# Threshold attention and a gated FFN on one core: half-size units of plain products, new slot tables, and one more dependency in the planner's account

## The chip, the cores and the metric

The kernel runs on one core of one Trainium2 chip, in float32. The metric is device time in microseconds of one execution. Times are medians of several runs; the profile is of one execution with its own time. "PE" is TensorE, "DVE" is VectorE, "ACT" is ScalarE, "POOL" is GpSimd, and "SP" is the sync engine, which issues most DMA transfers.

## What is computed

Attention over 8 batches of 8 heads with 576 positions of 64 elements, in which scores below the row's maximum less `tau` are dropped, and then a gated feed-forward block over the 4608 tokens (512 to 1536 to 512).

```python
def _attn_ref(q, k, v, tau):
    scale = 1.0 / np.sqrt(q.shape[-1])
    scores = scale * np.matmul(q, k.transpose(0, 1, 3, 2))
    thresh = np.max(scores, axis=-1, keepdims=True) - tau
    scores = np.where(scores >= thresh, scores, -1000000000.0)
    scores = scores - np.max(scores, axis=-1, keepdims=True)
    attn = np.exp(scores)
    attn = attn / (np.sum(attn, axis=-1, keepdims=True) + 1e-09)
    return np.matmul(attn, v)

def _moe_ref(x, w_gate, w_val, w_out):      # x: heads joined, 4608 x 512
    g = x @ w_gate
    silu = g * (1.0 / (1.0 + np.exp(-g)))
    val = x @ w_val
    return silu * val @ w_out
```

## The kernel before

The first 135 us are a head: the first batch's attention is done tile by tile, and the FFN's weights are loaded, converted and joined. After that the kernel is a run of 84 **slots**, 12 for each of the seven batches 1 to 7 (four head pairs times three groups of query rows). The FFN of batch b-1 runs inside the slots of batch b, and what is left over runs in a tail from about 1150 us on.

**One slot** is one round of the loop at the end of the kernel:

- `slot_scores` puts the score product on PE (line 1719, tile `sc`): 64 rows of the profile, written to two PSUM tiles of a pool of two, one for each head. So the next slot's scores can begin only when this slot's readers have let go of both tiles.
- `slot_rest` queues the softmax. DVE takes maxima (1740, 1742), the two halves of a row's maximum are joined either on DVE (1748, 1749) or on ACT (1754, then 1758 on DVE), ACT makes the threshold (1761) and six exps (1765), and DVE makes six masked products with their sums, the **masks** (1767). The masks are the last readers of the score tiles. Their six units are (head, u) for u = 0, 1, 2. Then sums are exchanged on ACT (1775), DVE makes the reciprocals (1780, 1781), ACT (1793) or POOL (1790) scales the units, and DVE transposes them (1795) for the product with V.
- In every third slot `attend` does that product for the head pair before (line 1816, tile `xa`). It waits for all nine transposes of its segment of three slots.
- `block_part` puts a share of the FFN's products on PE between this slot's scores and the next slot's. This share is what covers the softmax's latency.

**Which share a slot gets** is written in tables by slot number s (or by kk, the slot within a batch). For slots 0 to 8, `PLAIN` says how many steps of the generators `plain_group` are taken. These are the plain products of the first chunk (the FFN of batch 0): one step is one gate product `pg` or one value product `pv`, 8 matmuls of 128x128x256 (line 1200; float32 matmuls stand in the profile as two rows each, so 16 rows). `CH0` says how many output products `po` (line 1269, 12 rows each) slots 8 to 12 take. For slots 13 to 21, which carry the second chunk, `GV_FIRST` says how many products of `gates_and_values` (line 993, tiles `pa`, `pb`, `pe`, 8 rows each, a Strassen-like scheme of seven products for each of six groups) are taken. Later batches use `GV`, and from batch 3 on the output products are nested (line 1472, `px`, and 1481, `py`). `POOLED` and `FIRST_POOLED` say how many of a slot's scalings go to POOL, and `MAX_BY_ACT` and `FIRST_MAX_BY_ACT` list the slots whose maxima are joined on ACT. The "FIRST" tables hold for slots 0 to 23.

**What sets the order on the other engines** is `Plan`. PE's order is the order of the program. Every other instruction is a `job` with an engine, a planned duration, dependencies and a rank. Whenever PE work is added, `Plan.run` moves the account of time on and emits, engine by engine, the job that can start, lower rank first. Emitted order is final: each engine runs its queue in that order on the chip and waits where an operand isn't ready. The account's dependencies only decide the order; the waits that the program really has are put in by the framework from the tiles' accesses. In the account before, an exp of unit u = 2 follows the masks of u = 0 and 1 of its head, and an exp of u = 1 follows no mask.

`Deep.inner_sums` makes the sums of operands for the nested output products on POOL (line 846; `o` is the operand's number), and its jobs have rank 1 for o = 1 and 5 and rank 2 otherwise.

In slots 0 to 6 remaining pieces of the output weights are converted between the slots' jobs: ACT 873 and 876 (the first waits for the load of its piece, line 279 or 864), DVE 883 and 885, POOL 887.

Of the kernel before, what the change touches and what calls it, by code (L numbers as in the profile page):

```python
# [112 lines left out]
def kernel(  # L113
# [11 lines left out]
    nc = tc.nc  # L125
    P = 128
# [3 lines left out]
    NCC = DM // P  # L130
# [58 lines left out]
    wgv = big[:, 0:2 * NCC * DFF].rearrange("p (m c f) -> p m c f", m=2, c=NCC)  # L189
# [588 lines left out]
    job, pe = plan.job, plan.pe  # L778
# [194 lines left out]
    MM = 0.4325  # L973
# [215 lines left out]
    def plain_group(t, g, n_bufs):  # L1189

        x = xts["full", t]

        def mul(mat, name):
            hold = take(name)

            def fn():
                ps = hold.rows()
                for i in range(2):
                    for c in range(NCC):
                        nc.tensor.matmul(ps[:, i], wgv[:, mat, c, (2 * g + i) * P:(2 * g + i + 1) * P], x[:, c, :],  # L1200
                                         start=(c == 0), stop=(c == NCC - 1))

            return hold, pe(2 * NCC * MM, fn, *hold.deps)

        hold, m = mul(0, "pg")
        (u, u_old), (n, n_old) = turn_of(u_bufs), turn_of(n_bufs)
        ps = hold.rows()
        tj = job("ACT", 0.6, lambda: nc.scalar.activation(n.ap, ps, AF.Tanh, scale=0.5), m, *n_old, rank=1)
        cj = job("ACT", 0.6, lambda: nc.scalar.activation(u.ap, ps, AF.Copy, scale=0.5), m, *u_old, rank=1)
        hold.read_by(tj, cj)  # L1210
        hold.done(False)
        yield
        hold, m = mul(1, "pv")
        ht, pv = hall[:, t, g], hold.rows()
        vj = job("DVE", 0.7, lambda: nc.vector.scalar_tensor_tensor(out=ht, in0=n.ap, scalar=1.0, in1=pv, op0=ALU.add, op1=ALU.mult),
                 tj, m, rank=1)
        n.jobs = [vj]
        hold.read_by(vj)
        hold.done(False)
        gated[0, t, g] = mj = job("POOL", 1.3, pool_tt(ht, ht, u.ap, ALU.mult), vj, cj, rank=1)  # L1220
        u.jobs = [mj]
        yield
# [178 lines left out]
    class Deep:  # L1401
# [43 lines left out]
        def inner_sums(self, o, a, place, ready, *deps):  # L1445

            a11, a21, a12, a22 = quarters(a)
            flat = place if len(place.shape) == 2 else place.rearrange("p f n -> p (f n)")
            s1, s2, s3, s4 = (flat[:, n * QW:(n + 1) * QW].rearrange("p (f q) -> p f q", q=P) for n in range(4))
            tt, eng, took = (dve_tt, "DVE", 0.49) if tail[0] else (pool_tt, "POOL", 1.0)  # L1450
            rank = 1 if o in (1, 5) else 2
            j3 = job(eng, took, tt(s3, a11, a21, ALU.subtract), *ready, *deps, rank=rank)
            j1 = job(eng, took, tt(s1, a21, a22, ALU.add), *ready, *deps, j3, rank=rank)
            j2 = job(eng, took, tt(s2, s1, a11, ALU.subtract), j1, rank=rank)
            j4 = job(eng, took, tt(s4, a12, s2, ALU.subtract), j2, rank=rank)
            self.inner[o] = [(a11, ready), (a12, ready), (s4, [j4]), (a22, ready), (s1, [j1]), (s2, [j2]), (s3, [j3])]
# [267 lines left out]
    def slot_rest(seg, t, pss, mark, pooled, max_by_act, rank):  # L1724
        m = 2 * NU3
        mx, nm, th, ri, tot = statistics("mx", "nm", "th", "ri", "tot")
        sm = sums[0]
        sums.rotate(1)
        old_sums, sum_users[0] = sum_users[0], []
        sum_users.rotate(-1)  # L1730
        tiles = [(h, u) for u in range(NU3) for h in range(2)]
        at_of = lambda h, u: seg["p"] + (2 * (NU3 * t + u) + h) * SH
        scs = {(h, u): pss[h][:, u, 0:SH] if u < 2 else pss[h][:, :, SH:SH + SQ] for h, u in tiles}
        flat = {x: pall[:, at_of(*x):at_of(*x) + SH] for x in tiles}
        ps = {x: y if x[1] < 2 else y.rearrange("p (a n) -> p a n", a=2) for x, y in flat.items()}
        n_of = lambda h, u: NU3 * h + u
        rs = []
        for h, tile_ in enumerate(pss):
            n = n_of(h, 0)
            rs.append(job("DVE", 0.72, lambda n=n, tile_=tile_: nc.vector.tensor_reduce(  # L1740
                out=mx[:, n:n + 2, 0], in_=tile_[:, :, 0:SH], axis=AX.X, op=ALU.max, negate=True), mark, rank=0))
            rs.append(job("DVE", 0.42, lambda n=n, tile_=tile_: nc.vector.tensor_reduce(  # L1742
                out=mx[:, n + 2:n + 3, 0], in_=tile_[:, :, SH:SH + SQ], axis=AX.XY, op=ALU.max, negate=True), mark, rank=0))

        def largest():
            for g in range(NG):
                o = g ^ 1
                nc.vector.tensor_reduce(out=mx[g * G:(g + 1) * G, 0:m, 1], in_=mx[o * G:(o + 1) * G, 0:m, 0:1], axis=AX.X, op=ALU.max)
            nc.vector.tensor_reduce(out=nm[:, 0:m], in_=mx[:, 0:m, :], axis=AX.X, op=ALU.min)

        def others():
            for g in range(NG):
                o = g ^ 1
                nc.scalar.copy(mx[g * G:(g + 1) * G, 0:m, 1], mx[o * G:(o + 1) * G, 0:m, 0])

        if max_by_act:
            oj = job("ACT", 0.78, others, *rs, rank=0)
            nj = job("DVE", 0.18, lambda: nc.vector.tensor_reduce(out=nm[:, 0:m], in_=mx[:, 0:m, :], axis=AX.X, op=ALU.min), oj, rank=0)
        else:
            nj = job("DVE", 0.82, largest, *rs, rank=0)  # L1760
        ej = job("ACT", 0.25, lambda: nc.scalar.activation(th[:, 0:m], nm[:, 0:m], AF.Identity, bias=cut, scale=-1.0), nj, rank=0)
        masks = {}
        for h, u in tiles:
            x, n = (h, u), n_of(h, u)
            ej = job("ACT", 0.42, lambda x=x, n=n: nc.scalar.activation(ps[x], scs[x], AF.Exp, bias=nm[:, n:n + 1]), ej,  # L1765
                     *((masks[h, 0], masks[h, 1]) if u == 2 else ()), rank=0)
            masks[x] = job("DVE", 0.45, lambda x=x, n=n: nc.vector.scalar_tensor_tensor(  # L1767
                out=ps[x], in0=scs[x], scalar=th[:, n:n + 1], in1=ps[x], op0=ALU.is_ge, op1=ALU.mult, accum_out=sm[:, n, 0:1]),
                ej, *old_sums, rank=0)
        sc_users[:] = masks.values()  # L1770

        def exchange():
            for g in range(NG):
                o = g ^ 1
                nc.scalar.copy(sm[g * G:(g + 1) * G, 0:m, 1], sm[o * G:(o + 1) * G, 0:m, 0])  # L1775

        xj = job("ACT", 0.78, exchange, *masks.values(), rank=1)

        def total():
            nc.vector.tensor_reduce(out=tot[:, 0:m], in_=sm[:, 0:m, :], axis=AX.X, op=ALU.add)  # L1780
            nc.vector.reciprocal(out=ri[:, 0:m], in_=tot[:, 0:m])  # L1781

        rj = job("DVE", 0.36, total, xj, rank=1)
        sum_users[-1].append(rj)
        for u in range(NU3):
            scaled = []
            for h in range(2):
                x, n = flat[h, u], n_of(h, u)
                if h and u < pooled:
                    scaled.append(job("POOL", 1.02, lambda x=x, n=n: nc.gpsimd.tensor_scalar(  # L1790
                        out=x, in0=x, scalar1=ri[:, n:n + 1], scalar2=None, op0=ALU.mult), rj, rank=1))
                else:
                    scaled.append(job("ACT", 0.46, lambda x=x, n=n: nc.scalar.activation(x, x, AF.Copy, scale=ri[:, n:n + 1]), rj, rank=rank))  # L1793
            both = pall[:, at_of(0, u):at_of(0, u) + 2 * SH]
            seg["turned"].append(job("DVE", 0.72, lambda both=both: nc.vector.transpose(out=both, in_=both), *scaled, rank=rank))  # L1795
# [118 lines left out]
    NS = NU3 * NP  # L1914
    LAST_GV, LAST_PLAIN = 9, 8
    GV = {1: 2, 2: 7, 3: 4, 4: 5, 5: 6, 6: 5, 7: 6, 8: 6, 9: 0}
    GV_FIRST = {1: 4, 2: 5, 3: 4, 4: 6, 5: 7, 6: 3, 7: 5, 8: 6, 9: 1}
    CH = {0: 2, 1: 3, 10: 4, 11: 4}
    POOLED = {1: 3, 3: 2, 6: 3, 7: 2, 11: 1}
    MAX_BY_ACT = (0, 3, 5, 6, 8, 9, 10)  # L1920
    FIRST_POOLED = {0: 2, 1: 2, 4: 1, 6: 1, 7: 2, 8: 2, 10: 1, 11: 1, 12: 2, 13: 2, 14: 3, 15: 3, 17: 2, 18: 1, 19: 3, 20: 1, 21: 1, 22: 1, 23: 3}
    FIRST_MAX_BY_ACT = (0, 1, 2, 3, 6, 9, 12, 15, 16, 18, 20, 21)
    CD = {0: 1, 1: 1, 9: 2, 10: 2, 11: 2}
    PLAIN = {0: 2, 1: 2, 2: 3, 3: 1, 4: 2, 5: 3, 6: 1, 7: 2}
    CH0 = {8: 3, 9: 2, 10: 4, 11: 3, 12: 2}

    def begin_outputs(c):
        if c < DEEP:
# [39 lines left out]
    for s, (n, x) in enumerate((n, x) for n in range(len(halved)) for x in range(NU3)):  # L1968
        seg = halved[n]
        i, t = seg["i"], seg["tiles"][x]  # L1970
# [30 lines left out]
        if s in WS:  # L2001
            g, place = WS[s]
# [75 lines left out]
```

## Time and profile before

| | us |
|---|---|
| median of 3 runs (1369.13 to 1370.78) | 1370.28 |
| the profiled execution | 1371.92 |
| its span, first to last instruction | 1369.8 |
| PE, of the chain that ended last | 89% |
| mean granted TensorE clock | 0.997 |

The chain that ended last is PE for nearly nine tenths; its largest lines are the products of `gates_and_values` (993, 39% in three tiles), the nested products (1472, 12%), the scores (1719, 10%) and `xa` (1816, 9%). The plain products of line 1200 are 4%. PE's busy share by fortieths of the span is 89 to 96% over the first 171 us and 97 to 100% from there to the last slice. A timeline's row has start, duration, engine, line, operation and tiles, and in brackets the engine's idle time before it with what ended it. A row's duration on PE is not its cost where rows overlap; the distance of starts is.

### The profile page before, as it was taken

To read this page: it belongs to the slowest core of one execution; us is meant where nothing else is said; L and a number is where in the kernel's file an instruction comes from. 1 tells how busy PE (TensorE), PEld (TensorE's weight loads), DVE (VectorE), ACT (ScalarE), POOL (GpSimd) and SP (SyncE) were. 2 spreads that over 40 slices of the span, in tenths; PEclk is the share of its full clock that TensorE was granted. 3 is DMA by queue.
4 is the path that set the end of the run, shared out by engine and by line. 5 is a ranking of instruction groups with operands and counts; after the bars stand their busy time and mean duration, and the time that the engine had idled before them with its cause. 6 is when DMAs were issued, how large, how long until landed. Compare 5 with 4: busy or idle time off the path is not lost.

```text
span 1369.8 us, 39206 instructions
## 1 busy us (share of the span) xinstructions
PE 1350.8 (99%) x15590; PEld 1120.1 (82%) x15590; DVE 1069.4 (78%) x2815; ACT 876.6 (64%) x2277; POOL 717.6 (52%) x665
## 2 busy tenths in 40 slices
PE   9899999999999999999999999999999999999998
PEld 7777787778778778887888888878887788999998
DVE  6788888887887777777778877877777776788786
ACT  6798777666756767676767766776767774330330
POOL 1689597664564669534974287437943592000000
PEclk9999999999999999999999999999999999999999
DMA  7762424455523541555154513553165403424411
GB/s 168 185 204 74 103 55 124 133 137 144 174 52 126 144 116 38 171 147 141 36 157 130 151 47 128 139 144 92 37 191 144 113 27 136 161 78 147 151 65 32
DMA packets 208294, 162.32 MB, mean 119 GB/s; under 512 B 166128, under 2 KB 180464, under 8 KB 202736
## 3 DMA queue, kind: packets, MB, share of 16 engines
q1 hardware_dynamic: 203920, 158.86, 41.1%
q8 instruction: 124, 2.03, 0.6%
q10 hardware_dynamic: 4192, 0.95, 0.3%
q14 instruction: 58, 0.48, 0.1%
HBM read 138.28 MB, written 21.50 MB: 117 GB/s over the span
## 4 chain that ended last, share of the span: by engine, by line
PE 89%; DVE 4%; DMA 2%; POOL 2%; issue 1%; SPq 1%; ACT 1%; ACTq 0%; DVEq 0%; POOLq 0%
PE pb L993 18%; PE pa L993 12%; PE px L1472 12%; PE sc L1719 10%; PE xa L1816 9%; PE pe L993 9%; PE po L1269 5%; PE py L1481 5%; PE pg L1200 2%; PE pv L1200 2%; PE sc L1154 2%; SPq L367 1%; DMA vall<-in_v_dram 1%; PE pe L1154 1%; PE sc L438 1%
## 5 line engine op out<-in xcount | busy, mean ns | idle before, releaser
L1767 DVE SCALAR_TENSOR_TENSOR pall<-sc,th,pall 128x288 f32<-128x288 f32 x504 | 244.1, 514 | 59.3 <-ACT pall L1765 44.1
L993 PE MATMUL pb<-xall,big 128*128 128x256 f32 x1152 | 273.6, 381 | 0.0
L1765 ACT ACTIVATE pall<-sc,nm 128x288 f32<-128x288 f32 x504 | 231.4, 496 | 34.9 <-DVE pall L1767 34.8
L993 PEld LDWEIGHTS pb<-xall,big 128*128 128x128 f32 x1152 | 216.9, 191 | 30.5 <-issue 2.5
L1795 DVE STREAM_TRANSPOSE pall<-pall 128x576 f32<-128x576 f32 x252 | 188.9, 763 | 51.3 <-ACT pall L1793 34.6
L1793 ACT ACTIVATE pall<-pall,ri 128x288 f32<-128x288 f32 x415 | 189.4, 527 | 26.4 <-DVE ri L1781 25.8
L846 POOL TENSOR_TENSOR hall<-hall,tmp 128x512 f32<-128x512 f32 x80 | 102.2, 1277 | 158.5 <-DVE hall L1046 141.7
L993 PE MATMUL pa<-xall,big 128*128 128x256 f32 x768 | 183.5, 382 | 0.0
L993 PEld LDWEIGHTS pa<-xall,big 128*128 128x128 f32 x768 | 143.3, 190 | 21.8 <-issue 3.4
L1740 DVE TENSOR_REDUCE mx<-sc 128x2 f32<-128x576 f32 x168 | 125.0, 744 | 35.6 <-PE sc L1719 35.1
L1719 PE MATMUL sc<-kT,qT 64*32 64x288 f32 (+1 forms) x5376 | 147.4, 345 | 3.0 <-DVE pall L1767 1.4
L1719 PEld LDWEIGHTS sc<-kT,qT 64*32 64x32 f32 x5376 | 96.6, 106 | 56.9 <-issue 19.8
L993 PE MATMUL pe<-xall,big 128*128 128x256 f32 x576 | 137.3, 382 | 0.1
L1816 PE MATMUL xa<-pall,vall 64*32 64x288 f32 x4032 | 129.0, 404 | 0.1
L993 PEld LDWEIGHTS pe<-xall,big 128*128 128x128 f32 x576 | 108.7, 190 | 16.9 <-issue 2.9
L1790 POOL TENSOR_SCALAR pall<-pall,ri 128x288 f32<-128x288 f32 x89 | 88.7, 1007 | 63.9 <-DVE ri L1781 60.7
L1816 PEld LDWEIGHTS xa<-pall,vall 64*32 64x32 f32 x4032 | 75.8, 107 | 45.6 <-issue 5.3
L1775 ACT COPY sums<-sums 32x6 f32<-32x6 f32 x336 | 66.6, 198 | 41.3 <-DVE pall L1767 36.6
L1045 ACT ACTIVATE vall<-tmp 128x512 f32<-128x512 f32 x96 | 60.2, 630 | 28.8 <-POOL tmp L846 10.7
L1481 PE MATMUL py<-wo,hall 128*128 128x256 f32 x336 | 74.8, 380 | 0.0
L1742 DVE TENSOR_REDUCE mx<-sc 128x1 f32<-128x288 f32 x168 | 74.7, 445 | 0.0
L846 POOL TENSOR_TENSOR tmp<-tmp 128x512 f32<-128x512 f32 x36 | 45.9, 1274 | 53.6 <-ACT tmp L1068 53.6
(258 smaller groups left out, 2485.1 us busy)
## 6 DMA issues: line engine op xcount, KB each, us to landing
big<-sums_hbm SPq DMA_DIRECT2D x42, 1024.0 KB, 5.2
big<-sums_hbm SPq DMA_DIRECT2D x48, 768.0 KB, 4.8
vall<-in_v_dram SPq DMA_DIRECT2D x112, 144.0 KB, 3.1
out_dram<-big SPq DMA_DIRECT2D x32, 256.0 KB, 2.8
qT<-in_q_dram SPq DMA_DIRECT2D x112, 72.0 KB, 4.7
kT<-in_k_dram SPq DMA_DIRECT2D x112, 72.0 KB, 3.1
wo<-in_moe_w_gate_dram SPq DMA_DIRECT2D x16, 384.0 KB, 4.0
wo<-in_moe_w_val_dram SPq DMA_DIRECT2D x16, 384.0 KB, 4.7
```

Of the source, the lines that this page charges most:

```text
L846: return lambda: nc.gpsimd.tensor_tensor(out=out, in0=a, in1=b, op=op)
L993: nc.tensor.matmul(ps[:, i], w[:, k_, i * P:(i + 1) * P], x[:, k_, :], start=first and i == k_ == 0, stop=True, skip_group_check=True)
L1472: nc.tensor.matmul(ps, a[:, f, :], ws[n][:, f, :], start=bank_ not in begun, stop=True, skip_group_check=True)
L1481: nc.tensor.matmul(ps(), a[:, f, i * P:(i + 1) * P], operands[o][:, f, :], start=first and f == 0, stop=True, skip_group_check=True)
L1719: nc.tensor.matmul(pss[h][(slice(g * G, (g + 1) * G), *part)], qT[hs, col:col + G], kT[hs, c * SH + keys[0]:c * SH + keys[1]], start=True, ...
L1740: rs.append(job("DVE", 0.72, lambda n=n, tile_=tile_: nc.vector.tensor_reduce(out=mx[:, n:n + 2, 0], in_=tile_[:, :, 0:SH], axis=AX.X, op= ...
L1765: ej = job("ACT", 0.42, lambda x=x, n=n: nc.scalar.activation(ps[x], scs[x], AF.Exp, bias=nm[:, n:n + 1]), ej, *((masks[h, 0], masks[h, 1] ...
L1767: masks[x] = job("DVE", 0.45, lambda x=x, n=n: nc.vector.scalar_tensor_tensor(out=ps[x], in0=scs[x], scalar=th[:, n:n + 1], in1=ps[x], op0 ...
L1790: scaled.append(job("POOL", 1.02, lambda x=x, n=n: nc.gpsimd.tensor_scalar(out=x, in0=x, scalar1=ri[:, n:n + 1], scalar2=None, op0=ALU.mul ...
L1793: scaled.append(job("ACT", 0.46, lambda x=x, n=n: nc.scalar.activation(x, x, AF.Copy, scale=ri[:, n:n + 1]), rj, rank=rank))
L1795: seg["turned"].append(job("DVE", 0.72, lambda both=both: nc.vector.transpose(out=both, in_=both), *scaled, rank=rank))
L1816: nc.tensor.matmul(holds[a].ap()[x * G:(x + 1) * G, 0:SH].rearrange("d (i q) -> d i q", q=G), vr[rs, h, j, ds], p[rs, h, :, j, :], start=( ...
```

## The change

- `plain_group` hands out its two products in halves: `mul` makes one of the two rows i of the PSUM tile (4 matmuls), and the generator yields between them, so that a step of the plain stage is half as long as before. The waits on the PSUM bank stand on the first half.
- `PLAIN` counts halves now (32 in all, for 16 products before) and is laid out anew. `CH0` starts in slot 7 and takes one less in slot 10. `GV_FIRST`, `FIRST_POOLED` and `FIRST_MAX_BY_ACT` have other entries; `GV_FIRST` has 41 steps as before.
- In the planner's account, an exp of unit u follows the mask of unit u-1 of its head: for u = 1 that is new, for u = 2 the mask of u = 0 is no longer named.
- In `Deep.inner_sums`, o = 1 has rank 0 (before: 1).

```diff
@@ plain_group
-        def mul(mat, name):
-            hold = take(name)
-
+        def mul(hold, mat, i):
             def fn():
                 ps = hold.rows()
-                for i in range(2):
-                    for c in range(NCC):
-                        nc.tensor.matmul(ps[:, i], wgv[:, mat, c, (2 * g + i) * P:(2 * g + i + 1) * P], x[:, c, :],
-                                         start=(c == 0), stop=(c == NCC - 1))
-
-            return hold, pe(2 * NCC * MM, fn, *hold.deps)
-
-        hold, m = mul(0, "pg")
+                for c in range(NCC):
+                    nc.tensor.matmul(ps[:, i], wgv[:, mat, c, (2 * g + i) * P:(2 * g + i + 1) * P], x[:, c, :],
+                                     start=(c == 0), stop=(c == NCC - 1))
+
+            return pe(NCC * MM, fn, *(() if i else hold.deps))
+
+        hold = take("pg")
+        mul(hold, 0, 0)
+        yield
+        m = mul(hold, 0, 1)
...
-        hold, m = mul(1, "pv")
+        hold = take("pv")
+        mul(hold, 1, 0)
+        yield
+        m = mul(hold, 1, 1)
@@ Deep.inner_sums
-            rank = 1 if o in (1, 5) else 2
+            rank = 0 if o == 1 else 1 if o == 5 else 2
@@ slot_rest
             ej = job("ACT", 0.42, lambda x=x, n=n: nc.scalar.activation(ps[x], scs[x], AF.Exp, bias=nm[:, n:n + 1]), ej,
-                     *((masks[h, 0], masks[h, 1]) if u == 2 else ()), rank=0)
+                     masks.get((h, u - 1)), rank=0)
@@ tables
-    GV_FIRST = {1: 4, 2: 5, 3: 4, 4: 6, 5: 7, 6: 3, 7: 5, 8: 6, 9: 1}
+    GV_FIRST = {1: 5, 2: 8, 3: 2, 4: 5, 5: 7, 6: 2, 7: 5, 8: 7, 9: 0}
...
-    FIRST_POOLED = {0: 2, 1: 2, 4: 1, 6: 1, 7: 2, 8: 2, 10: 1, 11: 1, 12: 2, 13: 2, 14: 3, 15: 3, 17: 2, 18: 1, 19: 3, 20: 1, 21: 1, 22: 1, 23: 3}
-    FIRST_MAX_BY_ACT = (0, 1, 2, 3, 6, 9, 12, 15, 16, 18, 20, 21)
+    FIRST_POOLED = {0: 2, 4: 1, 5: 1, 8: 1, 9: 1, 11: 2, 12: 2, 13: 3, 15: 3, 16: 3, 17: 2, 19: 2, 20: 2, 22: 3, 23: 3}
+    FIRST_MAX_BY_ACT = (1, 3, 6, 9, 10, 11, 12, 13, 14, 18, 20, 21)
...
-    PLAIN = {0: 2, 1: 2, 2: 3, 3: 1, 4: 2, 5: 3, 6: 1, 7: 2}
-    CH0 = {8: 3, 9: 2, 10: 4, 11: 3, 12: 2}
+    PLAIN = {0: 3, 1: 5, 2: 6, 3: 2, 4: 5, 5: 5, 6: 3, 7: 3}
+    CH0 = {7: 1, 8: 3, 9: 2, 10: 3, 11: 3, 12: 2}
```

## The prediction

> **What bounds the kernel now.** I read the page first, then who waited for whom on TensorE, then the timelines of PE, DVE and ACT over the first two main batches (135 to 420 us of the span).
>
> ```profile
> PE 1350.8 (99%) x15590; PEld 1120.1 (82%) x15590; DVE 1069.4 (78%) x2815; ACT 876.6 (64%) x2277; POOL 717.6 (52%) x665
> ```
>
> ```profile
> PE sc L1719 <- DVE pall L1767: 1.4, 2, 0.9
> PE sc L1719 <- issue: 1.2, 2, 0.7
> ```
>
> TensorE is the bound, and its recorded waits after the start are small. But "busy" hides stalls, so I measure from start to start. Here is the pair of slots 1 and 2 (start, duration, engine, line):
>
> ```profile
> 152.76 3.62 PE L1200 MATMUL pv<-xall,big 128*128 128x256 f32 x16
> 157.25 2.13 PE L1719 MATMUL sc<-kT,qT 64*32 64x288 f32 x64 [0.87 <-DVE pall L1767]
> 159.31 3.72 PE L1200 MATMUL pg<-xall,big 128*128 128x256 f32 x16
> 162.86 3.62 PE L1200 MATMUL pv<-xall,big 128*128 128x256 f32 x16
> 166.32 3.62 PE L1200 MATMUL pg<-xall,big 128*128 128x256 f32 x16
> ```
>
> From 162.86 to 166.32 sixteen rows took 3.46 us, 0.216 each, with nothing in between. The pv at 152.76 should have ended at 156.22; sc came at 157.25, 1.03 late. That sc then held PE for 2.06 (159.31-157.25) where an undisturbed one holds it 1.65 (169.86 to 171.51), 0.41 more. So this slot lost 1.43 us, though PE reads as nearly always busy. The reason is the loop of a slot: sc needs both PSUM tiles of the slot before, and they are free after its six masks (L1767). I call the time from a slot's first score matmul to its last mask its latency, and from one slot's first score matmul to the next's its period. PE stalls where the work between two sc is shorter than the latency. Slots 13 and 14 show it twice:
>
> ```profile
> 281.55 1.89 PE L993 MATMUL pb<-xall,big 128*128 128x256 f32 x8
> 283.55 0.64 PE L1719 MATMUL sc<-kT,qT 64*32 64x288 f32 x2
> 284.74 1.69 PE L1719 MATMUL sc<-kT,qT 64*32 64x288 f32 x62 [0.55 <-DVE pall L1767]
> 293.37 1.89 PE L993 MATMUL pe<-xall,big 128*128 128x256 f32 x8
> 295.32 2.35 PE L1719 MATMUL sc<-kT,qT 64*32 64x288 f32 x64
> 297.59 1.99 PE L993 MATMUL pa<-xall,big 128*128 128x256 f32 x8
> ```
>
> **The change part by part.** No matmul is added or removed: only the order differs, and on PE only in slots 0 to 21 (by the built instruction order). So the sum is stalls removed less stalls made.
>
> *Halves and tables (PLAIN, CH0, GV_FIRST): stalls removed.* A half is 8 rows, 8 x 0.216 = 1.73 us, like a product of L993. Slot 1 gets 5 halves for 4, slot 4 gets 5 for 4, slot 7 three halves and a po product (2.59) for 4 halves, slot 13 five products for 4, slot 14 eight for 5; slots 0, 5, 10, 15, 16, 18, 21 give them up (6 and 20 gain a unit too, without a stall to remove).
> - Slot 1: 1.43 lost, 1.73 more cover: removed 1.43.
> - Slot 3: pv 171.51+3.46 = 174.97, xa at 175.31, so 0.34 waiting for the last transpose of the segment; the next sc 1.86 for 1.65, 0.21. The transpose is now queued before L885 and slot 2 ends earlier: removed 0.55 (priced again below).
> - Slot 4: 185.08+3.46 = 188.54 against 188.81, 0.27, and sc 2.06, 0.41: 0.68.
> - Slot 7: 216.31+3.46 against 219.98, 0.21, and sc 0.40: 0.61; the cover added is 0.86.
> - Slot 13: 281.55+1.73 = 283.28 against 283.55, 0.27, and the sc to 286.36 took 2.81, 1.16: 1.43; cover added 1.73.
> - Slot 14: 293.37+1.73 = 295.10 against 295.32, 0.22, and sc 2.27, 0.62: 0.84; cover added 5.2.
> Sum removed: 5.54. The stall of 0.56 inside the sc of slot 19 ("issue") I don't count: no mask was due there, and a 16 KB instruction transfer is under way (346.22); matmul counts up to there are equal before and after.
>
> *Stalls made.* Slot 0 keeps 3 halves. In the run before:
>
> ```profile
> 139.68 1.33 DVE L883 TENSOR_SCALAR wo<-wo 128x768 uint32<-128x768 uint32 x1
> 145.68 0.51 DVE L1767 SCALAR_TENSOR_TENSOR pall<-sc,th,pall 128x288 f32<-128x288 f32 x1
> 145.94 0.93 ACT L873 ACTIVATE wo<-xall 128x768 f32<-128x768 f32 x1
> 146.72 1.72 PE L1719 MATMUL sc<-kT,qT 64*32 64x288 f32 x64
> ```
>
> The next sc would be due at 146.72-1.73 = 144.99. The maximum over the halves of a row moves to DVE (0.82 after the reduces' end at 139.7: 140.5), and ACT now runs th, two exps (to 141.8), then L873, then four exps. L873 waits for a load issued at 137.76; loads of that line took 4.3 to 4.8, so 142.1 to 142.6, plus 0.93: exps 3 to 6 and behind them masks 3 to 6 wait till 143.0 to 143.5. From there exp 0.44, mask 0.5, the dependent exp and mask once more and a last mask make some 2.3: last mask 145.3 to 145.8, and sc ends 1.75 after it, 147.05 to 147.55, against 144.99+1.65 = 146.64. Cost 0.4 to 0.9; I take 0.8, as L883 took 0.55 or 1.33 and can add more. The Trainium skill (SBUF — State Buffer, Who interferes with whom) says that a DVE operation in a two-port mode is blocked by a running POOL instruction for its whole length; L883's 1326 and 550 ns beside and without POOL work differ by less than POOL's 1.8 us. By that rule slot 0 would cost up to 1 us more, by the row 0.8 at most; the sum goes by the row.
>
> Others, period without a stall against latency: 1.65 + products + 0.1.
> - Slot 3: 9.6 against 9.6 before; L885 (0.96) now stands between the reduces and nm, in place of ahead of the reduces: 0.4 (0 to 0.8).
> - Slots 15 and 18: 1.65+2x1.73+4.39+0.15 = 9.65. The shortest latencies in the run are 8.72 with the maximum on DVE (slot 23) and 9.24 on ACT (slot 9). Both slots put hall<-pb (0.69) ahead of the masks, waiting for a product that ends 5.3 after the slot's start: first mask at 6.1, 3.5 for six: 9.6. I take 0.2 and 0.3 (0 to 0.9 each).
> - Slot 16: 10.4 against 10.1 (8.72 + exp delayed by one ACT copy 0.59 + a transpose 0.78): 0.2 (0 to 0.7). Slot 21: 10.45 against 10.2: 0.1 (0 to 0.6).
> Sum made: 0.8+0.4+0.2+0.3+0.2+0.1 = 2.0; low 0.4, high 4.8 (0.9 of it slot 0).
>
> *Pool and ACT lists (FIRST_POOLED 34 to 31 scalings, FIRST_MAX_BY_ACT 12 of 24 as before).* Three scalings move from POOL (1.0) to ACT (0.46); both engines idle in these slots (ACT 0.7 to 0.9 us waits between groups at 173 and 184), so nothing on the path beyond the latencies above. Without that cover it is 3 x 0.46 = 1.4.
>
> *The masks in the account.* The exps of second units really wait already: L1765 idles 0.20 for L1767 between the first and second pair in each slot I read. The instruction's wait stays; the planner now puts other ACT work (0.59 each) there. It reaches all 84 slots. From slot 24 on PE finds its sc free in all of them, with 0.6 us to spare at the least, in the sixth slot of every batch:
>
> ```profile
> 772.38 1.89 PE L993 MATMUL pa<-xall,big 128*128 128x256 f32 x8
> 773.07 0.52 DVE L1767 SCALAR_TENSOR_TENSOR pall<-sc,th,pall 128x288 f32<-128x288 f32 x1
> 774.20 1.59 PE L1719 MATMUL sc<-kT,qT 64*32 64x288 f32 x56
> ```
>
> There a transpose (0.77) moves from ahead of the reduces to between masks 2 and 3, where mask 3 waited for hall<-pb, which waits for PE until 770.9: it fits the idle 0.36+0.17 and the earlier reduces. I take 0 (-0.5 to +1.5 over five batches). *The rank of the second product's sums* moves three POOL sums ahead in the nested batches; the product behind them starts without a wait now: 0. If that cover were gone, it is one POOL sum (1.0) a batch.
>
> *A rule that speaks against any of this:* the Trainium skill (Perfetto Trace Analysis, Identifying the Most-Contended Engine) says matmul busy share doesn't tell how near the roof TensorE is, weight-load share does. By PEld's 82% an estimate of headroom is 250 us and no order of slots would matter much. The start-to-start spacing says otherwise here, and the sum goes by it.
>
> **Sum.** 1371.92 (the profiled execution; 2.1 of it outside its 1369.8 span) - 5.54 + 2.0 = 1368.4. The median of the runs is 1.64 below that execution: 1366.8.
>
> **Rivals.** *Cover moved, not gained*: the made stalls reach their high end, 4.8, or most of it: slots 0, 3, 15 and 18 were given the shortest covers of all. 1370.28-5.54+4.5 = 1369.2. For it: four periods within 0.1 of their latencies. Against: each has only one small operation in the way.
> *Everything removed and nothing made*: -5.54, 1364.7. For it: shortest latencies lie under every new period; against: slot 0's load.
> *Slower*: the new order costs the steady batches. Place: the sixth slot's DVE queue, 0.6 to spare; price: a transpose and hall<-pb ahead of the last masks not absorbed (0.77+0.69+0.5 for the exp behind them = 2.0) is 1.4 over, five times, 7.0: 1373.8. It decides from (3.5+2.7)/5 = 1.25 us a batch. For it: ACT's order changes in every such slot. Against: DVE there does the same work, started 0.7 earlier.
> *It doesn't do what it says* (stalls are not from masks): 1370.3. Against: the recorded releaser is L1767 both times.
>
> **How the numbers follow.** Forecast 0.52, nothing made 0.12, cover moved or no effect 0.24, slower 0.12. About 0.2% (2.7 us) is what a measurement of this kernel can tell from no change. Forecast and "nothing made" fall below 1367.5 but for 0.02 of theirs: faster 0.62. Same: 0.25, slower: 0.13, as a weaker slow case falls in the one and small losses in the other. The range goes from 1364.6 (nothing made) to 1370.6 (cover moved and 1 us lost); the forecast's own is 1365.4 to 1368.2.
>
> **What would show it.** Right: sc at the ends of slots 1, 4, 7, 13, 14 comes 3.46 or 1.73 after the last product's start and holds PE 1.65; slot 0's period has a stall near 0.8 behind L873; from slot 24 on periods are those of before, shifted by some 3.5 us. Wrong: L1719 waits for L1767 in slots 3, 15, 18 by more than 0.5 each, or any of the sixth slots grows.

## The result, and the profile after

| | us |
|---|---|
| before, median of 6 runs (1368.72 to 1372.0) | 1370.01 |
| after, median of 6 runs (1363.65 to 1365.92) | 1365.1 |
| ratio, 95% interval | 0.9963, 0.995 to 0.9976 |
| the profiled execution after, and its span | 1365.92, 1363.7 |

The kernel is 4.9 us faster, by the interval 3.3 to 6.9. The forecast was 3.5 faster.

The page of the changed kernel, engines' busy time, shows almost nothing:

```profile
PE 1347.7 (99%) x15590; PEld 1115.2 (82%) x15590; DVE 1067.5 (78%) x2815; ACT 881.6 (65%) x2280; POOL 713.8 (52%) x662
```

The same number of matmul rows, the same shares. What PE waited for by the profile (line, releaser, total, times, longest) has changed a little:

```profile
PE sc L1722 <- DVE pall L1770: 0.8, 1, 0.8
PE sc L1722 <- issue: 0.8, 2, 0.4
```

(L1722 and L1770 are the scores and the masks, lines 1719 and 1767 of before.) One wait for a mask is left. The timeline of PE at the end of slot 1 (start, duration) answers to the first one shown of before:

```profile
152.68 3.62 PE L1197 MATMUL pv<-xall,big 128*128 128x256 f32 x16
156.23 1.72 PE L1722 MATMUL sc<-kT,qT 64*32 64x288 f32 x64
157.87 3.72 PE L1197 MATMUL pg<-xall,big 128*128 128x256 f32 x16
```

152.68 + 3.46 = 156.14, so sc comes 0.09 later and holds PE for 1.64: nothing is lost where 1.43 was. The ends of slots 13 and 14, in the timeline of all engines:

```profile
281.35 1.89 PE L993 MATMUL pe<-xall,big 128*128 128x256 f32 x8
...
282.68 0.51 DVE L1770 SCALAR_TENSOR_TENSOR pall<-sc,th,pall 128x288 f32<-128x288 f32 x1
283.17 1.86 PE L1722 MATMUL sc<-kT,qT 64*32 64x288 f32 x64
284.96 1.99 PE L993 MATMUL pb<-xall,big 128*128 128x256 f32 x8
...
297.15 1.89 PE L993 MATMUL pb<-xall,big 128*128 128x256 f32 x8
298.97 1.72 PE L1722 MATMUL sc<-kT,qT 64*32 64x288 f32 x64
300.62 1.56 PE L993 MATMUL pa<-xall,big 128*128 128x256 f32 x6
```

Slot 13's last mask ends at 283.19, as sc starts: 0.14 is lost (284.96-283.17 for 1.65), not 1.43. Slot 14 loses nothing. Slot 0 is where the change loses time:

```profile
136.36 0.37 SPq L279 DMA_DIRECT2D xall<-in_moe_w_out_dram  x1
...
141.47 0.92 ACT L873 ACTIVATE wo<-xall 128x768 f32<-128x768 f32 x1 [1.13 <-DMA xall<-in_moe_w_out_dram]
...
141.77 1.89 PE L1197 MATMUL pv<-xall,big 128*128 128x256 f32 x8
142.28 0.89 ACT L1768 ACTIVATE pall<-sc,nm 128x288 f32<-128x288 f32 x2
...
144.35 0.51 DVE L1770 SCALAR_TENSOR_TENSOR pall<-sc,th,pall 128x288 f32<-128x288 f32 x1
144.49 2.14 PE L1722 MATMUL sc<-kT,qT 64*32 64x288 f32 x64 [0.83 <-DVE pall L1770]
...
146.56 0.69 PE L539 MATMUL xa<-big,vall 128*64 128x64 f32 x16
```

ACT stands 1.13 in L873 for a load, and exps 3 to 6 behind it begin at 142.28. PE could have begun the scores at 141.77+1.73 = 143.50; they begin at 144.49 and take 2.07: 0.99+0.42 = 1.41 lost. The sixth slot of a late batch, the place of the slower rival, in the same view:

```profile
768.45 0.52 DVE L1770 SCALAR_TENSOR_TENSOR pall<-sc,th,pall 128x288 f32<-128x288 f32 x1
769.58 1.72 PE L1722 MATMUL sc<-kT,qT 64*32 64x288 f32 x64
```

Last mask's start to scores is 1.13, as before (773.07 to 774.20).

To see where the time went I divided each profile at the starts of the first score row of certain slots. "Steady" is the sum of the stretches between slots 22 and 40, 44 and 67, 74 and 83; "end" is all from slot 83 on. Each row is one profiled execution.

| profile | head, to slot 0 | slots 0-12 | 13-21 | 40-43 | 67-73 | steady | end |
|---|---|---|---|---|---|---|---|
| before | 135.18 | 139.45 | 107.91 | 50.89 | 82.08 | 614.93 | 239.32 |
| before, again | 130.99 | 139.22 | 107.65 | 50.88 | 81.35 | 614.91 | 239.72 |
| after | 133.77 | 138.42 | 106.26 | 50.34 | 81.36 | 614.96 | 238.60 |
| after, again | 130.85 | 138.24 | 106.61 | 50.19 | 81.35 | 614.91 | 238.60 |
| second chunk's tables of before | 132.29 | 137.84 | 108.29 | 50.37 | 81.72 | 614.93 | 238.59 |
| account alone | 132.41 | 138.47 | 109.88 | 50.60 | 81.68 | 616.06 | 238.60 |
| rank alone | 135.59 | 139.32 | 107.67 | 50.88 | 81.80 | 614.93 | 238.84 |
| account and rank alone | 131.07 | 138.46 | 108.57 | 50.91 | 81.81 | 614.97 | 238.59 |
| after without the account | 132.26 | 140.40 | 105.89 | 50.86 | 81.74 | 614.97 | 238.59 |
| after, later landing | 135.19 | 136.83 | 105.80 | 50.82 | 81.99 | 614.93 | 238.59 |
| after, later landing, again | 132.39 | 136.83 | 105.99 | 50.63 | 81.63 | 614.92 | 238.59 |
| whole products | 130.31 | 145.23 | 105.66 | 51.08 | 81.98 | 614.93 | 239.91 |
| whole products, later landing | 130.85 | 140.11 | 105.85 | 51.39 | 81.80 | 614.92 | 239.31 |

The first and third rows differ by 1.4 in the head, where no instruction differs; the head ranges over 5.3 us in these profiles and follows the granted clock (last section), so that is no gain of the change. By the means of the two profiles each, slots 0 to 21 give 2.35 (247.12 to 244.77), and three places where the prediction expected nothing give 1.9: slots 40 to 43 0.62, 67 to 73 0.36, the end 0.92. These are two executions of each kernel; that the medians hold the same parts is not shown.

### The profile page after: what moved, and what is told of

It reads as the page before. It is cut to its first block, busy times and chain, and to the rows that moved or that the text cites. A ratio compares the mean times of both kernels' runs of the same rounds, so it can differ in the third digit from the quotient of the medians.

```text
span 1363.7 us, 39192 instructions
## 1 busy us (share of the span) xinstructions
PE 1347.7 (99%) x15590; PEld 1115.2 (82%) x15590; DVE 1067.5 (78%) x2815; ACT 881.6 (65%) x2280; POOL 713.8 (52%) x662
## 4 chain that ended last, share of the span: by engine, by line
PE 91%; DVE 3%; POOL 2%; DMA 2%; issue 1%; SPq 1%; ACT 0%; ACTq 0%; DVEq 0%; POOLq 0%
PE pb L993 18%; PE pa L993 12%; PE px L1475 12%; PE sc L1722 10%; PE xa L1819 9%; PE pe L993 9%; PE po L1272 5%; PE py L1484 5%; PE pv L1197 2%; PE pg L1197 2%; PE sc L1154 2%; PE pe L1154 1%; SPq L367 1%; PE sc L438 1%; PE sc L1475 1%
## 5 line engine op out<-in xcount | busy, mean ns | idle before, releaser
L1770 DVE SCALAR_TENSOR_TENSOR pall<-sc,th,pall 128x288 f32<-128x288 f32 x504 | 244.0, 513 | 59.7 <-ACT pall L1768 43.1
L1722 PE MATMUL sc<-kT,qT 64*32 64x288 f32 (+1 forms) x5376 | 145.8, 346 | 1.7 <-DVE pall L1770 0.8
L1722 PEld LDWEIGHTS sc<-kT,qT 64*32 64x32 f32 x5376 | 94.7, 106 | 55.9 <-issue 20.2
L1793 POOL TENSOR_SCALAR pall<-pall,ri 128x288 f32<-128x288 f32 x86 | 85.2, 1003 | 82.1 <-DVE ri L1784 81.3
```

What stands on the lines that cost most here:

```text
L1722: nc.tensor.matmul(pss[h][(slice(g * G, (g + 1) * G), *part)], qT[hs, col:col + G], kT[hs, c * SH + keys[0]:c * SH + keys[1]], start=True, ...
```

## The experiments

Times stand as ratios to the kernel before, run on the same chip in turn; its median was 1368.73, 1367.89 and 1368.46 us in the three sets.

**Both kernels again.** No edit.

> The kernel before, a second time, unchanged: a measure of what the profile and the times vary by themselves. Theory: the head up to the first scores of slot 0 takes anything from 132 to 136 us (the six profiles so far range from 132.29 to 135.59 with the same instructions in it), the stalls inside the scores of slots 19, 43, 67 and 73 come and go between 0 and 1.1 us each, the stalls at the ends of slots 1, 3, 4, 7, 13, 14 come back within 0.15 us, and so does the px stall of 0.62 in the tail. Rival (head and stalls inside scores belong to the kernel, and the change shortened them): head within 0.3 of 135.18, the stalls within 0.2 of those of the first profile.

Measured: 1367.6 us against 1367.89, ratio 1.0001 (0.9989 to 1.0013). The head took 130.99 where it had taken 135.18. The stalls at the ends of slots 1, 4, 7, 13 and 14 came back, slot 1's 0.23 shorter than before and the others as they were; the stall inside the scores of slot 43 was 1.13 (1.05 before), those of slots 67 and 73 were gone; the tail's stall, where a nested product waits for a sum of DVE (line 849), came back with 0.83.

> The changed kernel, a second time, unchanged. Theory: the same stall of 1.4 (1.2 to 1.6) at slot 0 behind L873, 0.4 at slot 3, none at slots 1, 4, 7, 14; the segment of slots 0 to 21 within 0.5 us of 244.7, the head free between 132 and 136; median 4 to 5 us below before. Rival (the stall at slot 0 depends on the load's landing in that one execution): below 0.7 or above 2.

Measured: 1362.72, ratio 0.9965 (0.9952 to 0.9978). Slot 0 lost 0.79+0.41 = 1.20, slot 3 0.40, slots 0 to 21 took 244.85. So the stall at slot 0 is the kernel's and not that execution's, and the gain of 4.9 repeats (0.9965 of 1367.89 is 4.8 less).

**The second chunk's tables undone.**

```diff
-    GV_FIRST = {1: 5, 2: 8, 3: 2, 4: 5, 5: 7, 6: 2, 7: 5, 8: 7, 9: 0}
+    GV_FIRST = {1: 4, 2: 5, 3: 4, 4: 6, 5: 7, 6: 3, 7: 5, 8: 6, 9: 1}
```

(and the entries for slots 13 to 23 of `FIRST_POOLED` and `FIRST_MAX_BY_ACT`)

> The changed kernel with the second chunk's tables of before (GV_FIRST, and the entries of FIRST_POOLED and FIRST_MAX_BY_ACT for slots 13 to 23); plain stage, account and rank stay changed. Theory (a slot stalls where its cover is shorter than its softmax): the stalls of slots 13 and 14 come back, 2.0 to 2.3 us over the changed kernel, so 1367.1 to 1367.4 if the kernel before takes 1370.0; the two stalls show at those slots with L1770 as releaser, and slots 15 to 21 are as short as in the changed kernel. Rival (the gain of slots 13 to 21 was not from covers but from where instruction transfers fall): within 0.5 us of the changed kernel.

Measured: 1366.11, ratio 0.998 (0.9969 to 0.999). PE's timeline at slot 13:

```profile
279.32 0.64 PE L1722 MATMUL sc<-kT,qT 64*32 64x288 f32 x2
280.56 1.69 PE L1722 MATMUL sc<-kT,qT 64*32 64x288 f32 x62 [0.60 <-DVE pall L1770]
282.18 2.00 PE L993 MATMUL pe<-xall,big 128*128 128x256 f32 x8
```

The scores start, stand after two rows and take 2.86 in all (279.32 to 282.18), 1.2 more than undisturbed, with the mask as releaser. Slot 14 loses 0.38+0.62 again, and slots 13 to 21 are 1.7 to 2.0 longer than after, the removed stalls. The theory holds for `GV_FIRST` and the two lists together; the lists were never changed by themselves, so their share is not shown. The rest of the change is worth 2.7 us by itself (0.2% of 1368.73; by the interval 1.4 to 4.2).

**The account alone, on the kernel before.**

```diff
-                     *((masks[h, 0], masks[h, 1]) if u == 2 else ()), rank=0)
+                     masks.get((h, u - 1)), rank=0)
```

> The kernel before with the account's line alone changed: an exp of unit u follows the mask of unit u-1 of its head. Prediction on record: 0 (-0.5 to +1.5). Theory from the two traces: the changed kernel gained 1.2 us in steady slots 40, 43, 67, 73 at stalls that no semaphore releases, and 0.6 in the tail; these are not the account's but a matter of where instruction loads fall, so this kernel is within 0.5 us of before, the sixth slots of the batches keep their periods. Rival one (the account frees the steady slots): 1.2 to 2.0 us faster. Rival two (the account costs the sixth slots): 1.0 to 7.0 us slower.

Measured: 1370.79, ratio 1.0014 (1.0002 to 1.0025): slower, and the first theory falls. The sixth slots are innocent. The steady stretches grow by 1.13, 0.28 in one slot of each nested batch, the larger part at one place of the nested products (all engines' timeline, batch 3):

```profile
535.67 1.50 PE L1472 MATMUL px<-big,hall 128*128 128x128 f32 x12
536.14 1.00 POOL L846 TENSOR_TENSOR hall<-hall 128x384 f32<-128x384 f32 x1
...
537.20 0.74 PEld L1472 LDWEIGHTS px<-wo,hall 128*128 128x128 f32 x6 [0.21 <-POOL hall L846]
537.20 0.94 PE L1472 MATMUL px<-wo,hall 128*128 128x128 f32 x6
```

The last six px rows wait for a sum that POOL ends at 537.14: 1.53 from start to start for 1.34. Slots 13 to 21 also took 2.0 more, 1.42 of it inside the scores of slot 13, with no releaser.

**The rank alone, and with the account, on the kernel before.**

```diff
-            rank = 1 if o in (1, 5) else 2
+            rank = 0 if o == 1 else 1 if o == 5 else 2
```

> The kernel before with the rank of the operand o=1 alone changed (0 for 1). Prediction on record: 0. Theory: within 0.4 us of before. Rival (the rank is what took the 0.62 us stall of a nested product px in the tail and 0.5 at a steady slot): 0.6 to 1.2 us faster, and the tail's px stall is gone.

Measured: 1367.81, ratio 0.9997 (0.9987 to 1.0007). No effect alone. The tail's stall was 0.14 here; the load behind it landed earlier in this profile (see the next section), and the kernel with the account alone, which has the rank of before, has no such stall either, so the rank is not shown to take it away.

> The kernel before with the account's line and the rank of o=1 changed, the tables and the plain products as before. Theory (the account alone let a POOL sum come late for a nested product, 0.28 us in each of the batches from 3 on, and the rank alone cures that): stretches 22-39, 44-66 and 74-83 at 221.88, 279.71, 113.34 again (221.87+0.29, +0.55, +0.29 with the account alone); slots 13 to 21 stay 1.5 to 2.2 us longer than before (the old table with the new order); in all 0 to 1.5 us above the kernel before. Rival (the loss of the account alone has another cause): the three stretches as with the account alone.

Measured: 1368.25, ratio 0.9999 (0.9986 to 1.0011). The steady stretches are at 614.97 again. The same products:

```profile
532.55 5.08 POOL L846 TENSOR_TENSOR big<-big 128x384 f32<-128x384 f32 x5
533.03 1.50 PE L1472 MATMUL px<-big,hall 128*128 128x128 f32 x12
534.37 0.83 PE L1472 MATMUL px<-wo,hall 128*128 128x128 f32 x6
```

The hall sum is no longer among the POOL sums of that moment, and the six rows follow after 1.34 without a wait. So the rank is worth nothing alone and 1.1 us beside the account: it pays for what the account breaks. Slots 13 to 21 were only 0.8 longer than before and not 1.5 to 2.2, since the stall in the scores of slot 13 was 0.35 here and 1.42 there.

**The changed kernel without the account.** The account's line as before.

> The changed kernel with the account's line of before (an exp of the third unit follows the masks of the first two, one of the second unit follows none); halves, tables and rank stay changed. Theory (the account moves work on DVE, ACT and POOL, and PE's steady slots have room for either order): slots 22 to 83 as in the changed kernel (221.88, 279.71 and 113.34 us in the three stretches without a stall inside scores), slots 0 to 21 shorter by 0.5 to 1.0 at slot 0 (L873 is queued after four exps and not after two) and otherwise within 1 us; in all within 1.5 us of the changed kernel. Rival (the account is what makes the new tables work): slots 13 to 21 longer by over 1.5 us, 2 us or more slower.

Measured: 1365.05, ratio 0.9975 (0.9964 to 0.9986), some 1.4 us behind the changed kernel's 0.9965, with intervals that overlap; the profile is clearer. Slot 0 loses nothing here (period 9.82 against 10.72 after), as L873 stands behind four exps, but slot 3, which neither theory nor rival named, does:

```profile
167.67 3.72 PE L1197 MATMUL pv<-xall,big 128*128 128x256 f32 x16
...
171.83 0.76 DVE L1798 STREAM_TRANSPOSE pall<-pall 128x576 f32<-128x576 f32 x1
...
172.69 5.06 PE L1819 MATMUL xa<-pall,vall 64*32 64x288 f32 x144 [1.30 <-issue]
...
178.49 0.92 PE L1722 MATMUL sc<-kT,qT 64*32 64x288 f32 x10 [0.74 <-DVE pall L1770]
```

xa begins 1.56 late (167.67+3.46 = 171.13), just after the ninth transpose, which DVE took behind L885 and four reductions. The wait is put down to "issue", but the transpose ending at 172.59 is the last thing that xa needs. The masks are late behind further pieces of the weights (L883 and L885, to 175.86), so the scores come 1.41 after xa's 4.39. Slots 0 to 12 take 2.1 more than after. So the account makes the stall of slot 0 in the changed kernel and saves a larger one by DVE's order in slot 3.

**L873 later in slot 0.** `landed` is the time at which the account takes the load that slot 0's L873 needs to have landed.

```diff
-        landed = 6.3
+        landed = 9.0
```

> The changed kernel with one number of the account changed: the load that L873 in slot 0 waits for is taken to have landed at 9.0 for 6.3, so that L873 is queued behind slot 0's six exps. PE's order is that of the changed kernel. Theory (the load ahead of exps 3 to 6 makes slot 0's stall of 1.4): the stall of slot 0 falls to 0 to 0.4, the time by 1.0 to 1.4 to 1363.7 to 1364.1. Rival (slot 0's three halves are too short in any case, or L873 is then late for slot 1 to 3): no gain, 1365.1, with the stall at slot 0 or moved to slots 1 to 3.

Measured: 1362.32, ratio 0.9956 (0.9942 to 0.9969). Slot 0's period is 9.82, 0.90 less than after, and no stall has moved to slots 1 to 3.

> The changed kernel with the planned landing at 9.0 for 6.3, a second time, beside the changed kernel on the same chip. Theory (its slots 0 to 21 are 2.0 us shorter than the changed kernel's: 242.63 against 244.68): 1.5 to 2.2 us below the changed kernel's median, slots 0 to 21 within 0.3 us of 242.6. Rival (the gain in the first run was the head's): within 0.6 us of the changed kernel.

Measured: 1363.09, ratio 0.9967 (0.9952 to 0.9981), beside 1362.72 for the changed kernel. The second run's slot 0, all engines:

```profile
140.39 1.89 PE L1197 MATMUL pv<-xall,big 128*128 128x256 f32 x8
...
140.87 0.94 ACT L1768 ACTIVATE pall<-sc,nm 128x288 f32<-128x288 f32 x2 [0.15 <-DVE pall L1770]
...
141.85 0.52 DVE L1770 SCALAR_TENSOR_TENSOR pall<-sc,th,pall 128x288 f32<-128x288 f32 x1
142.21 1.92 PE L1722 MATMUL sc<-kT,qT 64*32 64x288 f32 x64
143.67 0.92 ACT L873 ACTIVATE wo<-xall 128x768 f32<-128x768 f32 x1
```

With L873 behind the exps, sc starts 0.09 after its due time. Slots 0 to 21 took 242.63 and 242.82, 2.0 less than after; slot 3's stall is gone too. That the stall at slot 0 comes from L873 ahead of exps 3 to 6, its wait for the load and its own 0.92 together, is shown. That the kernel is faster than the changed one is not: 1.5 to 2.2 was expected, and the medians on the same chip are 0.4 apart the other way. Their profiles' heads were 132.39 and 130.85, and the mean granted clocks of their runs 0.9984 and 0.9989; by a straight line through the 23 runs of the kernel before on that chip (1.15 us for 0.001 of clock) that is an estimated 0.5 us. Whether more runs would show the rest stays open. It beats the kernel before in both sets.

**Whole products in the plain stage.** `PLAIN` as 4, 4, 6, 2, 4, 6, 2, 4.

> The changed kernel with whole products only: PLAIN 4, 4, 6, 2, 4, 6, 2, 4 halves for slots 0 to 7 in place of 3, 5, 6, 2, 5, 5, 3, 3. Theory (a half is worth what it covers): slot 0's stall of 1.4 goes; slot 1 had 1.35 to spare and loses 1.73, slot 4 1.52 less 1.73, so stalls of about 0.4+0.4 (the scores that follow a late mask run 0.4 longer) and 0.2+0.4 come back: -1.4+0.8+0.6 = 0, within 0.6 us of the changed kernel, and slower than the version with the later landing by 1.4 to 2.4. Rival (halves bring the gain as such): 1.5 us or more above the changed kernel.

Measured: 1372.24, ratio 1.0036 (1.0023 to 1.0048). By the total it agrees with the rival, but the place doesn't. Slot 0's stall was gone and slot 1 lost 0.59+0.40, about as expected; 6.6 us were lost in slot 6. DVE's timeline and PE's xa:

```profile
205.56 0.77 DVE L1798 STREAM_TRANSPOSE pall<-pall 128x576 f32<-128x576 f32 x1
```

```profile
198.05 3.72 PE L1197 MATMUL pv<-xall,big 128*128 128x256 f32 x16
206.54 6.24 PE L1819 MATMUL xa<-pall,vall 64*32 64x288 f32 x144 [4.77 <-ACT sums L1778]
```

xa was due at 201.51. The profile names ACT's copies of sums, which end at 206.49, but xa reads nothing of theirs; it reads nine transposes, and the ninth stands in DVE's queue behind all six masks of slot 6, to 206.33. That is 5.03 of the 6.6. The rest is the clock: it was granted at 1.00 up to 206.3, at 0.50 to 209.7 and at 1.00 again, and xa held PE for 5.93 (to 212.47) for 4.39. My theory looked at the covers alone and missed that a new table also reorders DVE. So I tried whole products in an order where no such transpose exists: `landed = 9.0` and `PLAIN` as 4, 4, 6, 2, 4, 6, 4, 2.

> The version with the planned landing at 9.0 and whole products only: PLAIN 4, 4, 6, 2, 4, 6, 4, 2 halves for slots 0 to 7 in place of 3, 5, 6, 2, 5, 5, 3, 3. Here no transpose that xa waits for is queued behind the masks of xa's own slot, which was so in slot 6 of the earlier kernel of whole products. Theory (a half covers 1.73): against the version with halves, slot 1 (1.71 to spare) breaks even or loses 0.3, slot 4 (0.37 to spare) loses 1.3 + 0.4, slot 7 (0.42 to spare) 1.3 + 0.4; slots 0 to 12 take 139.5 to 140.5 us against 136.83, so 2.7 to 3.7 more. Rival (halves are not needed once the order behind L873 and xa is right): slots 0 to 12 below 138.0.

Measured: 1367.78, ratio 0.9988 (0.9978 to 0.9998); slots 0 to 12 took 140.11, in the expected range, 3.3 more than with halves. Slot 1, PE:

```profile
148.44 3.62 PE L1197 MATMUL pv<-xall,big 128*128 128x256 f32 x16
152.63 2.13 PE L1722 MATMUL sc<-kT,qT 64*32 64x288 f32 x64 [0.57 <-DVE pall L1770]
```

0.73+0.41 lost behind the last mask (148.44+3.46 = 151.90; the scores held PE 2.06), and 0.63+0.41 at the end of slot 7. Slot 4 lost nothing, since its first exp came 1.0 earlier in the slot than in the version with halves (5.25 after the slot's start for 6.22); xa in slot 3 came 0.73 late for 0.20 instead, and 0.40 stood inside slot 7's own scores, with no mask due. The total was right, its parts half.

**Everything moved along TensorE's instruction stream.** On the changed kernel, 20 more of the idle matmuls that the program starts with.

```diff
-    run_idle(6)
+    run_idle(26)
```

> The changed kernel with 20 more idle matmuls at the very start of TensorE's program, which moves everything after them by 40 rows in TensorE's instruction stream and changes nothing else. Theory (the stalls inside the scores of slots 19 and 43 sit at a fixed place of the instruction stream, where its next 16 KB are not there yet): the longest gap inside these scores, now at row 37 of 64 in slot 19 and row 31 in slot 43, is gone from there (the place moves to before the scores, among 0.22 us products or into the xa product), and both scores take 1.65 to 1.8 us from start to start; other score products may get such a gap instead, between rows 24 and 64. Rival (these stalls belong to the slot, by a wait that the profile doesn't name): the gaps stay at rows 37 and 31, 0.6 to 0.8 us. The time grows by the idle matmuls themselves, 5 to 9 us.

Measured: one run, 1367.22, with a head of 136.76. PE's timeline of slot 19 before, after, and with the idle matmuls:

```profile
346.62 1.40 PE L1719 MATMUL sc<-kT,qT 64*32 64x288 f32 x36
348.58 0.71 PE L1719 MATMUL sc<-kT,qT 64*32 64x144 f32 x28 [0.56 <-issue]
```

```profile
342.74 1.40 PE L1722 MATMUL sc<-kT,qT 64*32 64x288 f32 x38
344.50 0.71 PE L1722 MATMUL sc<-kT,qT 64*32 64x144 f32 x26 [0.36 <-issue]
```

```profile
344.68 1.70 PE L1722 MATMUL sc<-kT,qT 64*32 64x288 f32 x64
...
493.08 1.41 PE L1722 MATMUL sc<-kT,qT 64*32 64x288 f32 x40
494.99 0.69 PE L1722 MATMUL sc<-kT,qT 64*32 64x144 f32 x24 [0.50 <-issue]
```

The gap in slot 19 is gone, and so are those of slots 13 and 43; a new one of 0.88 stands in slot 31, where the changed kernel had none. The head is 5.9 longer than the changed kernel's second one, as much as was expected of the idle matmuls. The other profiles say the same of the place: number the matmul rows of the program from its start, and every such gap in the fourteen profiles (over 0.23 us from one row's start to the next, inside a score product, with no mask due; slots 7, 13, 19, 31, 43 and 67) stands after a row whose number is 69 to 73 more than a multiple of 126. So these stalls belong to a place in the instruction stream and not to a slot.

## Why the prediction was right, and where it wasn't

- **Stalls removed, 5.54: right in kind, too large by some 0.9.** Slots 1, 4, 7 and 14 lose nothing now (0.1 at most), slot 13 0.14. But the sum counts each score from its due time, and an undisturbed one comes 0.09 after it (slots 1 and 14 above), so each of the six slots was priced 0.09 too high; the prediction has this 0.1 where it adds up periods and not here. By the periods, which need no due time, slots 1, 3, 4, 7, 13 and 14 together give 4.2 (4.3 and 4.05 in the two pairs of profiles), against 5.54 less the 0.4 made in slot 3. With the second chunk's tables undone, 13 and 14 come back, which shows the mechanism.
- **Slot 0, 0.8: mechanism right, size too small.** It measured 1.41 and 1.20 from the due time, 1.3 and 1.1 by the periods. The load took 5.1 from issue to L873's start (136.36 to 141.47) where I had taken 4.3 to 4.8 from other loads of that line, and from exp 3 to the last mask's end it was 2.6 (142.28 to 144.86) for 2.3. Moving L873 takes the stall away.
- **Slot 3, 0.4 made: right** (0.41). PE's timeline after:

```profile
170.08 3.72 PE L1197 MATMUL pv<-xall,big 128*128 128x256 f32 x16
173.73 4.59 PE L1819 MATMUL xa<-pall,vall 64*32 64x288 f32 x144
178.15 2.13 PE L1722 MATMUL sc<-kT,qT 64*32 64x288 f32 x64
180.21 2.00 PE L1197 MATMUL pg<-xall,big 128*128 128x256 f32 x8
```

  xa comes 0.20 after its due time, as in the version with the later landing, where nothing holds it up, so of the 0.34 before only 0.14 was a wait; that is gone. The scores hold PE for 2.06, 0.41 too long, behind the late masks. Together slot 3 loses about what it lost before, where 0.15 less was forecast.
- **Slots 15, 16, 18 and 21, 0.8 together: wrong.** None of them stalls. Their latencies are 9.23, 9.17, 9.16 and 10.03 from first score to last mask, against periods of 9.69, 10.46, 9.69 and 10.55. I had let the last mask of 15 and 18 end 9.6 after the start, by counting 3.5 for six masks from a first one at 6.1; they took 3.15, some 0.4 less.
- **Not foreseen in slots 0 to 21:** 0.49 and 0.75 inside the scores of slot 13, of the instruction-stream kind. Net of slots 0 to 21: -3.54 forecast, -2.35 measured (4.2 given, 1.2 lost at slot 0, 0.6 in the scores of slot 13).
- **Account at 0 and steady periods unchanged: right for the kernel, wrong for the reason.** The steady stretches agree within 0.05. But alone the account costs 1.1 there, and the rank, which I priced at 0, is what takes that cost away. I had named the cost for the case that the cover is gone (one POOL sum a batch, 1.0); it is 0.28 a batch. That the account would decide the order of L873 and of DVE in slots 0 and 3 I had not seen.
- **The rivals.** "Nothing made", 1364.7, is nearest to the result in number and is not what happened: 1.2 was made at slot 0. The result, 1365.1, lies just under the forecast's own 1365.4 to 1368.2. In the slow rival's place nothing moved: the last mask ends as early as before.
- **The number.** The measured 4.9 is more than the forecast 3.5 although slots 0 to 21 gave only 2.35. The rest stands at places that I had left out of the sum: slot 43's scores (0.62; 1.05 and 1.13 before, 0.60 and 0.45 after), slots 67 to 73 (0.36) and the end (0.92). So it is partly luck that the total comes near. The first two places are tied to PE's stream, and there the stalls vary between executions: those of slots 67 and 73 stand in one profile of before and not in the other, and slot 43's was 0.88 and 0.89 in the version with the later landing, which has the changed kernel's order on PE. In the end DVE waits for a load, and a nested product on PE behind it; timelines of DVE before and after:

```profile
1211.24 0.43 DVE L849 TENSOR_TENSOR pall<-big 128x256 f32<-128x256 f32 x1 [1.82 <-DMA big<-sums_hbm]
```

```profile
1204.88 0.43 DVE L849 TENSOR_TENSOR pall<-big 128x256 f32<-128x256 f32 x1 [0.77 <-DMA big<-sums_hbm]
```

  The load is issued 74.98 after slot 83's start in every profile. It landed 5.8 and 6.2 later in the two of before, 6.4 and 5.8 in the two of whole products, 5.3 in that of the rank alone, and 4.3 to 4.8 in all others. Why is open. These parts add up to 4.25; the last 0.65 is within the interval.
- **The rule weighed there** (the Trainium skill, Perfetto Trace Analysis, Identifying the Most-Contended Engine: weight-load share, beside the share of peak work, as the measure of headroom) read 82% before and 82% after. The start-to-start spacing found the stalls; the share saw none of them go.
- **L883 beside POOL.** The prediction held L883's 1326 ns against the other rule, as less than POOL's 1.8 us was added. The rows don't say that: in before L883 began at 139.68, 0.9 into a POOL operation of 138.78 to 140.58, so 0.9 of it was left, and L883 took 0.78 more than alone: no contradiction. In the changed kernel it starts at 139.15, as that operation ends (139.17), and takes 0.55, so slot 0 tests neither price.

## What to carry to other kernels

Where an engine waits for a chain that other work is meant to cover, compare chain and cover slot by slot from start to start; busy shares and listed waits hide most of the loss. Take the undisturbed distance from a slot that doesn't stall, not from the sum of its pieces: 0.09 a slot was 0.5 us here. A new table of covers also gives the planner's queues a new order, and the dear accidents come from there: a transfer's consumer ahead of the exps (1.4), a transpose behind the masks (6.6, of which 1.5 at half clock). Edits of one change can pay for each other, so an edit that is worth nothing alone is not proved useless, and a total that fits is no proof of its parts.

## What was not expected of the hardware

- TensorE's score products stall at fixed places of its instruction stream. The gaps inside them, with no mask due and 0.24 to 1.34 us from one row's start to the next, stay at the same row of the same slot in one kernel (after 36 and 38 rows in slot 19 above), left slots 13, 19 and 43 when 40 rows were put ahead, and lie on a grid of 126 rows. The trace has 124 instruction transfers of 16 KB on one queue for 15590 matmul rows, one for 125.7. That PE waits there for its instructions is argued from this spacing and not shown: the transfer of 346.22 in before ended at 347.17, ahead of slot 19's gap (347.74 to 348.58), and most scores that hold such a place show no gap. One kernel differs from run to run in the size (slot 13's scores were 0.49 and 0.75 too long).
- The head of 130.3 to 135.6 us varies by 5.3 from execution to execution with the same instructions, more than the whole change is worth; one profile each before and after would have credited the change with 1.4 of it. The granted clock sorts the heads. In the first profile of before it is 0.50 from 41.0 to 47.8 us, in the second 1.00 there. The four profiles with 6.8 us of half clock near 40 us have heads of 133.8 to 135.6, the four with 3.4 us 132.3 to 132.4, and the five with none 130.3 to 131.1.
- The half clock of whole products' slot 6, 3.4 us long, came after 5 us in which PE stood idle for the transpose. In the head of before, too, PE was busy for only 2.60 of the 6.00 us ahead of it, and for 4.04 in the second profile, where the clock stayed. That the idle time brings it is not shown here.
